# Outputs of the pair path stored by row tile from 128 partitions, four transfers a batch, in place of two transfers of 64 partitions

## Chip, cores and metric

The kernel runs on one core of one Trainium2 chip. The metric is the device time of one execution in microseconds (us); lower is better. A core has five engines with queues of their own: PE (matmul; weight loads are shown apart as PEld), DVE (vector), ACT (scalar), POOL (GpSimd) and SP (which here only issues transfers). Transfers between the large memory (DRAM) and the on-chip memory of 128 partitions run on 16 DMA engines that all issuers share.

## What is computed

For 8 batches of 576 rows: linear attention with 8 heads of 64 columns, and behind it an MLP mixer with a token part and a channel part.

```python
phi = lambda x: np.where(x > 0, x, np.exp(x) - 1.0) + 1.0
kv  = einsum('bhsd,bhse->bhde', phi(k), v);  z = sum(phi(k), axis=2)
x   = einsum('bhsd,bhde->bhse', phi(q), kv) / (phi(q) . z + 1e-6)   # heads side by side: [8, 576, 512]
u   = x + (relu(x^T @ w_tok1) @ w_tok2)^T                           # 576 -> 256 -> 576
out = u + relu(u @ w_ch1) @ w_ch2                                   # 512 -> 1536 -> 512, float32
```

## The kernel before

A row s of a batch is written as s = 9 p + t, with p from 0 to 63 and t from 0 to 8 (`out.rearrange("n (p t) d -> n p t d", t=9)`, called `outv`). A row tile r, from 0 to 3, holds t = 2r in partitions 0 to 63 and t = 2r + 1 in partitions 64 to 127; `half[0]` and `half[1]` are these two halves. The 64 rows with t = 8 of each batch are the tail; tails of two batches share one tile and are stored on their own (`mm4_tail_put`).

The eight batches overlap. Every step is registered under a name by `put(name, function, ...)`, and the string `ORDER` (L66), written out by hand, lists the names in the order in which their instructions are issued; each engine works through its own instructions in that order and waits on semaphores where data are not ready. Names begin with the batch. `L` is an input load on SP's queue (L228), `qT` and `uT` are DMA transposes on SP's queue (L335, L489), `kx`, `qx`, `ka`, `qa`, `v` prepare phi and v on ACT and DVE (L252, L256, L275), `K`, `n`, `f`, `g` are matmuls of attention and of the token part, `x` and `p` those of the channel part (L928 and L970), which are done as seven products of half-size blocks with sums before and after.

Batch 0 stores its row tiles from `obuf`, a float32 buffer of six slots of 512 columns, by `mm4_put` (names `0o0`, `0o1`): for each pair of row tiles one transfer from each half, L764. Batches 1 to 6 take the pair path: a product holds two row tiles at once, so slot r of `obuf` (slots 0 to 3) holds row tile r, and the steps write quarters. `pair_end` (names `eZ`, `eW`, `eY`, `eX`, on DVE, L1064) adds PSUM and u into rows d and d + 2, columns half c, with (d, c) = Z (0, 0), W (1, 1), Y (0, 1), X (1, 0). `pair_copy` (`c0` to `c2`, ACT, L1058) copies a product to a buffer `part[i]` (these buffers lie in `q_raw`, `w` and `part`), and `pair_more` (`hZ`, `hY`, `hW`, POOL, L1071) adds it to Z, Y or W. Then `pair_put` (name `o`, POOL, L1075) stores all four tiles, one transfer from each half:

```python
for e in range(2):
    nc.gpsimd.dma_start(out=outv[n, :, e:e + 7:2], in_=slots(f"{n}P", 4)[half[e]])
```

Rows 0 and 2 (d = 0) are complete after `hZ` and `hY`, rows 1 and 3 after `hW` and `eX`. The slots 0 to 3 are the same for all batches of the pair path, so the `e` steps of a batch wait until the transfers of the batch before have read them. Batch 7 has a path of its own: it adds into `obuf` by L984 and L1031 and stores through SP and ACT at the end.

Of the kernel before, what the change touches and what calls it, by code (L numbers as in the profile page):

```python
# [64 lines left out]

ORDER = """A2 A0 A1 A3 A4 A5 A6 A8 A9 A7 A10 A12 A13 A14 A11 A16 A17 A15 A19 A18 A21 A20 A22 A23 A24 A25 A26 A27 A28 A29  # L66
A30 A33 A31 A32 A35 A34 A36 A37 A38 1Lk0 A39 1Lk1 1Lv1 A40 1Lq0 A41 1Lq1 A42 1Lv0 A43 0ma0 At2 0ma1 At3 0ma3
0mb1 0mb0 0ma6 0r0 0mb3 0r1 1ka0 0ma7 1kx0 0ma2 0ma8 0mb6 1kb0 0mb2 0r3 0mb8 0mb7 0r6 0r8 0ma4 0r7 G21 0gt
1kx1 G22 0ma9 0gv 0ma10 0mb4 1ka1 0r2 0ma5 0r4 G11 0mb10 1kb1 0mb5 0r10 G23 0mb9 0r5 0ma11 0mb11 1qa0 1qx0 B0
0r9 0q0 B1 0r11 1qb0 B2 1qx1 1qa1 1Q00 1Q01 0q1 1Qc01 1v0 1Qc00 0q2 1qb1 1v1 1Q10 1Q11 1K 1Qc11 2Lq0 ws02  # L70
1Qc10 0q3 2Lq1 1Kc0 1Kc1 2Lv0 ws04 1n20 1n01 2Lk0 1nc20 0q4 2Lk1 1nc01 2Lv1 1n10 0q5 1nc10 1n00 0q6 1nc00 1n11
0q7 1nc11 2qx0 1n21 ws14 0q8 1nc21 1f0 2qx1 2qa0 1f1 wt2 3Lq0 G24 0q9 1fr1 2qb0 1fr0 0q10 2qa1 2v0 G12 1h01
2qb1 1h00 1hu01 2qT1 ws00 0q11 1hu00 0z1 2kx0 1h10 2qT0 ws10 0z0 1h11 1hu10 1t0 1hu11 1t1 3Lv0 ws24 1g2 1tc1
1tc0 1t2 3Lq1 1t3 1gu2 1ma9 1tc3 ws12 0z2 1ma1 1ma5 1tc2 1ma4 0z3 1mb1 2v1 0o1 1mb5 1r1 1ma7 2ka0 2kx1 1mb7
G01 3Lk0 1ma10 0o0 G03 3qx0 1mb4 2kb0 0ut 1ma2 2ka1 1r4 1mb10 wt0 3Lk1 1mb2 1r7 1ma3 3Lv1 1r2 2kb1 1mb9 1r10
1ma8 3qa0 0uc 1mb8 1r5 ws20 1r9 2K 1r8 1mb3 2Kc0 2Kc1 3qb0 1ma6 1r3 2n ws30 2nd 1mb6 T00 2o0 ws34 1r6 2n1
1ma11 Tr00 2o1 ws22 1mb11 2ne 3v0 2n0 1ma0 1mb0 3qa1 T01 4Lv0 1r0 2n2 ws32 1r11 1p10 3qx1 2f0 1w13 G02 Tr01
4Lq1 1w10 1p11 3kx1 3qb1 1p20 3ka0 3kx0 2f1 1w20 G14 2fr0 4Lk0 T02 1w23 3qT1 1w30 1p50 Tr02 3kb0 1p51 2fr1
3qT0 1c0 1w40 1p21 4qx1 2g1 3ka1 1c2 1eZ 1p60 3v1 G13 1p61 2gu1 2g0 1c1 3kb1 2uT1 1p31 2gu0 4kx0 1p30 3K 4qa1
2uT0 1p71 3Kc1 1eY 3Kc0 4v0 1p70 4qb1 4Lv1 4Lq0 3n 1hY 1eW 4Lk1 U00 3ne 5Lv0 3nd 1hZ U01 3n2 U02 3o0 1hW 3n1  # L80
1p40 3n0 2x01 2x11 2s1 3o1 1p41 V0 2y11 2x02 2y01 2s2 1eX 2x15 2x21 2s3 1o 2x12 2y21 2x16 2y12 2x06 2y16 2s4
2x05 2y06 2y02 2x17 2y15 4qa0 2x26 4qx0 2x25 2y17 2x07 G04 3f0 2y25 4qb0 2y05 4ka0 2y26 4qT1 2x14 2x03 2y07
2y14 2x13 3fr0 4qT0 3f1 2y13 4kb0 2x27 5Lq0 3fr1 2y03 2x23 5Lk0 2x04 2y27 2x22 2y04 4ka1 2x24 4kx1 2y22 3gt
3g1 2y23 2y24 2w10 2p20 2w12 2p10 2w20 3gu1 2p50 2p11 2w22 3uT1 2p51 3gt1 2c0 3g0 4v1 4kb1 2w30 2p60 2p61 3gu0
2p21 2c1 3gt0 3uT0 4K 2eZ 2p70 4Kc1 2c2 2w40 3ut 2p71 4Kc0 4n 2eW 5Lq1 2p30 4nd 2hW 5Lk1 4ne 2p31 5Lv1 4n0
2p41 2hZ 4o0 4n1 2p40 3x11 3s1 3x21 4o1 3y11 3s2 3x01 4n2 5kx0 3x16 3x12 2eY 3y21 T12 3s3 5v0 2eX 2hY 3x15
3y12 3x05 3y16 3x02 5ka0 2o 3y01 3x26 3y02 6Lk0 3x25 3x06 5kb0 3y25 W0 3x22 3y26 5ka1 3x23 3y06 3x17 3y22 3y15
3x27 3s4 3y05 3x07 3y17 5kx1 T11 3y27 3x03 3y07 Tr12 6Lk1 3x14 Tr11 3y03 3x24 5kb1 3x13 3y24 4f0 3y13 5qx0
5qa0 4f1 3y14 3y23 4fr0 5qb0 3x04 4fr1 T10 3w12 3y04 5qa1 4g0 Tr10 3w10 5v1 4g1 4gu0 5qx1 3p20 4gu1 4uT0 5K
6kx1 3p21 3w20 4uT1 5qb1 3p10 5Kc1 6kx0 3w22 3p11 5qT1 3eZ 3p50 3c0 6ka1 3p51 5Kc0 5qT0 3w40 U10 3c2 3w30 U11  # L90
6Lq0 6Lq1 6kb1 U12 4s1 6ka0 3p31 V1 3p30 7Lk0 4s2 6Lv1 3p61 3eY 6Lv0 3p60 6kb0 7Lk1 5n 3c1 5nd 3hY 3p71 5ne
3p70 5n0 3hZ 4x02 5o0 3eW 4x01 4x21 5n2 4y01 3hW 3p40 4y21 4y02 4x06 6qx0 5n1 4x05 4x26 4y06 6qa1 3p41 4y05
5o1 4x11 4s3 4x03 3eX 4y11 4x25 4y26 4s4 3o 4x07 4y03 6qx1 4x12 4y07 4x16 4x27 4y25 4y12 4x04 4y16 6qb1 5f0
4y04 6qa0 6v0 4x15 4y27 4x23 4w10 4y15 4x17 6qb0 5fr0 4x22 4y17 4x13 6qT0 4x24 4y23 4x14 4y24 4y13 6qT1 5f1
4y14 4y22 6v1 7ka1 4p20 4w12 4p21 5fr1 4w20 5g1 4w22 4p10 5gu1 4p11 5g0 4w40 5uT1 4c0 4eZ 5gt 6K 5gu0 4hZ 4p50
6Kc1 6Kc0 5gt1 5uT0 7kx1 4p51 5gt0 4p60 4c2 4w30 7Lv0 6n 7kx0 7Lq0 7kb1 4p61 7Lq1 6ne 7Lv1 4p30 6nd 4c1 6n2
4p31 4p71 6n0 4p70 4eY 5x11 6o1 5x02 6o0 5y11 5s1 5x12 4eW 5x01 5s2 5x15 5y01 4hW 6n1 4p40 7v0 5x16 5y12 4p41
5y16 7ka0 5x06 5y15 5s3 5x21 5y02 7F12 5x13 5y21 4eX 4hY 5x17 5y06 5x05 5y17 5x26 5y05 7kb0 4o 5x07 5y26 5x25
5y13 5x03 5y25 5s4 5x27 7qa0 7qx0 6f0 5y07 7v1 7qb0 5x14 6f1 7qa1 7qx1 5y27 5x04 6fr0 5y03 5x22 6fr1 5x23 7qb1
5y14 5x24 5y22 5y04 7qT1 7K 5y23 5p10 7Kc1 7Kc0 5w10 7qT0 5y24 6g0 5w30 6g1 5w12 5w20 5p20 6gu1 5p50 5p11 5w22  # L100
6uT1 6gu0 5p21 5c0 5p51 5eZ 6uT0 5p60 5c2 5w40 7n 5hZ 7nd 5p61 7ne 5p31 7n1 5c1 7F15 5p30 7o1 7o0 5p70 7n2
5p71 6s1 5eY 6x21 6x01 6s2 5hY 7n0 6x11 6y01 6x12 6y11 6x06 6y21 6s3 6x15 5eW 6y06 6x16 6x02 5hW 6y16 6x05
6y02 5p40 6y12 7F14 6x26 6s4 6y15 6x17 7F11 6x25 6y26 6x07 7F10 6y05 5p41 6y25 W1 6x13 5eX 6x03 6y07 6x23 7F13
6x27 6y03 6x22 5o 6x04 6y22 7f0 6y17 6y23 7f1 7fr0 6y27 6y04 6x14 6y13 7fr1 6x24 6y14 6w30 7g0 6y24 6w10 6p10
7gu0 7g1 6w12 7uT0 6p11 6w20 6p50 6w22 6c0 5ut 6p20 7gu1 6p51 7F2 7uT1 7gt 6p61 7gt0 6p60 6w40 7x12 6c1 7gt1
6p21 6c2 7F4 7ut 6p71 6eZ 7x11 6p70 7s1 6hZ 7x02 6eW 7x01 6p30 7y01 6hW 6p31 7y11 7y02 7x05 7s2 6p40 7y12 7y05
7s3 7x06 7s4 7x16 7y06 6eY 7x03 6p41 6hY 7x15 6eX 7c1 7y15 7F3 6o 7y16 7x21 7cr1 7y03 7x13 7y21 7x17 7c5 7y17
7x07 7x26 7y07 7x22 7y26 7x25 7y22 7x14 7x27 7y14 7x04 7y25 7c4 7y04 7y27 7cr5 7x23 7w10 7cr4 7x24 7y23 7c3
7y24 7w30 7w20 7c2 7y13 7w14 7c0 7cr2 7w12 7w40 7cr3 7p50 7w34 7cr0 7w22 7p51 7w24 7w42 7p10 7w44 7ts1 7p11
7ta1 7R11 7R51 7p20 7w32 7t5 7R10 7ts2 7R50 7p61 7tb1 7p31 7R61 7ts4 7R20 7p30 7R31 7tr5 7p60 7tr1 7ts3 7p71  # L110
7R60 7p21 7t6 7R21 7R30 7p70 7R71 7D200 7tr6 7t3 7D711 7D710 7ta2 7D201 7tr3 7D210 7R70 7tb2 7p41 7D311 7tr2
7D310 7t7 7D211 7R41 7td20 7p40 7D411 7tr7 7D410 7t4 7td21 7R40 7D700 7D701 7tr4 7td70 7td71"""


@with_exitstack
def kernel(
# [20 lines left out]
    nc = tc.nc  # L137
# [23 lines left out]
    def bank(name):  # L161
        return psum[:, BANK[name]]
# [47 lines left out]
    half = [slice(0, 64), slice(64, 128)]  # L210
# [27 lines left out]
    def put(name, fn, *a):  # L238
        assert name not in tok, name
        tok[name] = lambda: fn(*a)  # L240
# [4 lines left out]
    def slots(name, m):  # L245
        return obuf[:, SLOT[name]:SLOT[name] + m]
# [504 lines left out]

    outv = out.rearrange("n (p t) d -> n p t d", t=T)

    def mm4_read(p, t):
        b, r = divmod(t, R)
        if t < 8:
            o, y = slots(f"0o{r // 2}", 2)[:, r % 2], u[b][:, r, :]
        else:
            o, y = slots(f"V{p}", 1)[:, 0], ut[p % 2]
        nc.vector.tensor_tensor(out=o, in0=bank(f"U{p}{t}"), in1=y, op=ALU.add)  # L760

    def mm4_put(i):
        for e in range(2):
            nc.gpsimd.dma_start(out=outv[0, :, 4 * i + e:4 * i + e + 3:2],  # L764
                                in_=slots(f"0o{i}", 2)[half[e]])

    def mm4_tail_put(p):
        for b in range(2):
# [10 lines left out]
    for r in range(R):  # L779
        put(f"0z{r}", mm4_read, 0, r)  # L780
    for i in range(2):
        put(f"0o{i}", mm4_put, i)
    for p in range(2):
        for i in range(3):
            put(f"U{p}{i}", mm4, p, 8, range(4 * i, 4 * i + 4))
        put(f"V{p}", mm4_read, p, 8)
        put(f"W{p}", mm4_tail_put, p)
# [282 lines left out]
        o = slots(f"{n}P", 4)[:, d::2, HC[c]]  # L1070
        nc.gpsimd.tensor_tensor(out=o, in0=o, in1=part[i], op=ALU.add)  # L1071

    def pair_put(n):
        for e in range(2):
            nc.gpsimd.dma_start(out=outv[n, :, e:e + 7:2], in_=slots(f"{n}P", 4)[half[e]])  # L1075

    for n in range(1, B - 1):
        for i in range(3):
            put(f"{n}c{i}", pair_copy, n, i)
        for z in "WZYX":  # L1080
            put(f"{n}e{z}", pair_end, n, z)
        for z, i in zip("WZY", (2, 0, 1)):
            put(f"{n}h{z}", pair_more, n, z, i)
        put(f"{n}o", pair_put, n)


    zeros = raw["v", 1].rearrange("p j f -> p (j f)")[:, 0:512]
# [110 lines left out]
```

## Time and profile before

| | us |
|---|---|
| median of 3 runs (244.76, 245.8, 245.11) | 245.11 |
| span of the profiled execution, first to last instruction | 243.4 |
| PE busy | 233.1 |
| DVE busy | 211.5 |
| ACT busy | 136.4 |
| POOL busy | 81.2 |
| one put of `pair_put` on POOL (12 of them), from issue to landing, median | 6.0 |
| issue of one such put, busy time of POOL | 0.634 |

The profile shows one execution; no separate time is given for it beside its span. Queue q0 is that of the transfers which POOL issues, q1 and q10 those of SP and ACT. DMA shares are means over the 16 engines. "Landing" is when the semaphore of a transfer reaches its full count. A wait is put down to what ended it last; "issue" is time in which an engine waited for nothing that the profile shows. The granted clock of PE is full in all forty slices.

### The profile page before, as it was taken

What the parts mean: (1) busy time and instruction counts of PE and PEld (TensorE: products, weight loads), DVE (VectorE), ACT (ScalarE), POOL (GpSimd) and SP (SyncE); (2) the same over time, 40 slices, a digit from 0 to 9 for tenths busy, and PEclk for the clock granted to TensorE, in tenths of its full rate; (3) what the DMA queues carried; (4) which work ended last, traced back from release to release, by engine and by line L of the source; (5) the groups of instructions that cost most, each with busy time, mean ns of one, the idle gap of its engine ahead of it and who ended that gap; (6) DMA issues with size and microseconds to landing.
All of it is one profiled execution on the core that took longest, in us unless ns stands there. A gap on an engine that the chain in (4) does not pass through costs nothing.

```text
span 243.4 us, 6361 instructions
## 1 busy us (share of the span) xinstructions
PE 233.1 (96%) x2597; PEld 174.2 (72%) x2616; DVE 211.5 (87%) x387; ACT 136.4 (56%) x224; POOL 81.2 (33%) x88
## 2 busy tenths in 40 slices
PE   7889989999999999999999999999999999999991
PEld 3575445464677686789867887688778867888881
DVE  5955786999999989999999999999999599867661
ACT  4773782669788277327994297448923542347000
POOL 8870044076910620035200520206015810440730
PEclk9999999999999999999999999999999999999999
DMA  6999989999979989978948989495782285143035
GB/s 230 278 202 260 317 260 234 409 283 286 365 225 198 270 265 161 247 97 305 285 127 175 370 262 200 82 260 178 161 138 40 44 171 112 24 91 81 3 80 180
DMA packets 49805, 48.42 MB, mean 199 GB/s; under 512 B 30064, under 2 KB 35568, under 8 KB 49776
## 3 DMA queue, kind: packets, MB, share of 16 engines
q1 hardware_dynamic: 41664, 35.00, 51.3%
q0 software_dynamic: 7472, 12.22, 25.5%
q10 hardware_dynamic: 640, 0.79, 1.0%
q8 instruction: 20, 0.33, 0.6%
q14 instruction: 9, 0.07, 0.1%
HBM read 35.85 MB, written 9.44 MB: 186 GB/s over the span
## 4 chain that ended last, share of the span: by engine, by line
PE 84%; DMA 9%; POOL 3%; issue 1%; DVE 1%; SPq 1%; POOLq 0%; DVEq 0%
PE ps L970 27%; PE ps L928 23%; PE ps L747 6%; PE ps L448 6%; DMA q_raw<-in_q_dram 5%; PE ps L459 4%; PE ps L686 4%; DMA wc<-in_moe_w_ch_dram 4%; PE ps L711 2%; PE ps L733 2%; PE ps L302 2%; PE ps L1024 2%; PE ps L387 2%; POOL qT L1111 1%; POOL cr L233 1%
## 5 line engine op out<-in xcount | busy, mean ns | idle before, releaser
L970 PE MATMUL ps<-k_raw,v_raw 128*128 128x256 bf16 x252 | 31.8, 273 | 0.0
L943 ACT COPY v_raw<-ps 128x512 f32<-128x512 f32 x30 | 17.0, 595 | 22.7 <-PE ps L928 21.5
L970 PEld LDWEIGHTS <-cr 128*128 128x128 bf16 x252 | 24.4, 98 | 4.8
L970 PEld LDWEIGHTS <-v_raw 128*128 128x128 bf16 x252 | 24.1, 98 | 3.8 <-issue 0.4
L928 PEld LDWEIGHTS <-swc 128*128 128x128 bf16 x240 | 23.4, 98 | 3.1
L681 DVE CUSTOM_DVE_ANT_0 cr<-ps,v_raw 128x512 bf16<-128x512 f32 x30 | 20.1, 684 | 4.5 <-PE ps L928 2.5
L928 PEld LDWEIGHTS <-wc 128*128 128x128 bf16 x216 | 21.1, 98 | 3.6
L928 PE MATMUL ps<-crt,swc 128*128 128x256 bf16 x180 | 23.1, 273 | 0.0
L252 ACT ACTIVATE e<-q_raw 128x1152 bf16<-128x1152 f32 x16 | 18.7, 1167 | 6.7 <-DMA q_raw<-in_q_dram 6.7
L686 PE MATMUL ps<-uT,wc 128*128 128x512 bf16 x91 | 21.6, 379 | 0.4 <-issue 0.2
L970 PE MATMUL ps<-wc,cr 128*128 128x256 bf16 x168 | 21.6, 273 | 0.0
L1071 POOL TENSOR_TENSOR obuf<-obuf,w 128x512 f32<-128x512 f32 x6 | 8.2, 1360 | 38.6 <-ACT w L1058 19.5
L252 ACT ACTIVATE e<-k_raw 128x1152 bf16<-128x1152 f32 x16 | 18.5, 1166 | 3.2 <-DMA k_raw<-in_k_dram 2.6
L1071 POOL TENSOR_TENSOR obuf<-obuf,q_raw 128x512 f32<-128x512 f32 x6 | 8.2, 1374 | 35.6 <-DVE obuf L1064 35.6
L928 PE MATMUL ps<-uT,wc 128*128 128x256 bf16 x144 | 19.5, 273 | 0.0
L1064 DVE TENSOR_TENSOR obuf<-ps,u 128x512 f32<-128x512 f32 x24 | 16.4, 685 | 2.5 <-PE ps L970 2.4
L1071 POOL TENSOR_TENSOR obuf<-obuf,part 128x512 f32<-128x512 f32 x6 | 7.7, 1289 | 26.5 <-DVE dens L400 18.5
L413 DVE TENSOR_TENSOR x<-ps,dens 128x768 bf16<-128x768 f32 x18 | 16.6, 930 | 0.0
L686 PEld LDWEIGHTS <-wc 128*128 128x128 bf16 x96 | 8.9, 98 | 10.0 <-issue 0.6
L470 DVE TENSOR_TENSOR u<-ps,x 128x1024 bf16<-128x1024 f32 x12 | 14.6, 1220 | 0.1
L836 DVE TENSOR_TENSOR v_raw<-cr 128x512 bf16<-128x512 bf16 (+3 forms) x24 | 14.5, 620 | 0.0
L448 PE MATMUL ps<-x,w 128*128 128x512 bf16 x50 | 13.9, 379 | 0.3
(168 smaller groups left out, 514.3 us busy)
## 6 DMA issues: line engine op xcount, KB each, us to landing
k_raw<-in_k_dram SPq DMA_DIRECT2D x16, 576.0 KB, 6.8
q_raw<-in_q_dram SPq DMA_DIRECT2D x16, 576.0 KB, 6.3
v_raw<-in_v_dram SPq DMA_DIRECT2D x14, 576.0 KB, 7.6
out_dram<-obuf POOLq DMA_DIRECT2D x12, 512.0 KB, 6.0
wc<-in_moe_w_ch_dram POOLq DMA_DIRECT2D x8, 384.0 KB, 9.3
out_dram<-obuf POOLq DMA_DIRECT2D x4, 256.0 KB, 7.3
cr<-in_v_dram POOLq DMA_DIRECT2D x2, 288.0 KB, 7.6
out_dram<-obuf POOLq DMA_DIRECT2D x4, 128.0 KB, 4.8
```

Source lines behind the costliest of these rows:

```text
L252: nc.scalar.activation(out=ebuf[EBUF[f"{n}{nm}{c}"]], in_=f, func=AF.Exp)
L413: nc.vector.tensor_tensor(out=xv[:, :, rc0:rc0 + 3], in0=nd_tile(n, m)[:, :, k0:k0 + 6, 0:D].rearrange("p i (q a) d -> p i q a d", a=2), i ...
L448: nc.tensor.matmul(out=banks(f"{n}f")[:, mt], lhsT=w1t[:, b, ms] if r == R else w1[:, r, ms], rhs=x[b][:, r, :], start=(r == 0), stop=(r = ...
L470: nc.vector.tensor_tensor(out=u[b][:, rs], in0=banks(f"{n}g{i}"), in1=x[b][:, rs], op=ALU.add)
L681: nc.vector._custom_dve(TENSOR_ADD_SAT, out=o, in0=ps, in1=c, s0=3.4028234663852886e38, s1=0.0)
L686: nc.tensor.matmul(out=bank(f"{n}m{mc}"), lhsT=wc1[:, kj, 128 * mc:128 * mc + 128], rhs=uTj[b][:, kj] if n < 2 - U1 else uT[b][:, :, kj], ...
L747: nc.tensor.matmul(out=bank(f"U{p}{t}"), lhsT=crt[:, kc, :] if t == 8 else cr[b][:, kc, 128 * r:128 * r + 128], rhs=wc2[:, kc, :], start=( ...
L928: nc.tensor.matmul(out=ps[:, j], lhsT=lhs[:, k_, 128 * j:128 * (j + 1)], rhs=rhs[:, :, k_], start=(first and j == 0 and k_ == 0), stop=(k_ ...
L943: nc.scalar.copy(out={1: c1, 6: c6, 5: c5}[i], in_=ps)
L970: nc.tensor.matmul(out=ps, lhsT=lhs[:, k_], rhs=rhs[:, k_], start=(first and not skip and k_ == 0), stop=(k_ == KH - 1), skip_group_check= ...
L1064: nc.vector.tensor_tensor(out=slots(f"{n}P", 4)[:, d::2, HC[c]], in0=pair_tile(n, "X" if z == "W" else z), in1=u[n % 2][:, d::2, HC[c]], o ...
L1071: nc.gpsimd.tensor_tensor(out=o, in0=o, in1=part[i], op=ALU.add)
```

## The change

One function now stores one row tile from all 128 partitions: the output side walks the two halves e, then p, then the columns. Batch 0 calls it for its four tiles (four transfers, as before), batches 1 to 6 for each tile as well (four transfers in place of two). For the pair path the name `o` becomes `oa` (rows 0 and 2) and `ob` (rows 1 and 3).

```diff
+    def put_rows(n, r, rows):
+        nc.gpsimd.dma_start(out=outv[n, :, 2 * r:2 * r + 2].rearrange("p e d -> e p d"), in_=rows)
+
     def mm4_put(i):
-        for e in range(2):
-            nc.gpsimd.dma_start(out=outv[0, :, 4 * i + e:4 * i + e + 3:2],
-                                in_=slots(f"0o{i}", 2)[half[e]])
+        for r in (2 * i, 2 * i + 1):
+            put_rows(0, r, slots(f"0o{i}", 2)[:, r % 2])
...
-    def pair_put(n):
-        for e in range(2):
-            nc.gpsimd.dma_start(out=outv[n, :, e:e + 7:2], in_=slots(f"{n}P", 4)[half[e]])
+    def pair_put(n, d):
+        for r in (d, d + 2):
+            put_rows(n, r, slots(f"{n}P", 4)[:, r])
...
-        put(f"{n}o", pair_put, n)
+        for d in range(2):
+            put(f"{n}o{'ab'[d]}", pair_put, n, d)
```

In `ORDER` each `no` (n from 1 to 6) becomes `nob` in the same place, and `noa` is put directly behind the later of `nhZ` and `nhY`; all other names keep their order. For batch 3:

```diff
-3p70 5n0 3hZ 4x02 5o0 3eW ...  3eX 4y11 4x25 4y26 4s4 3o 4x07
+3p70 5n0 3hZ 3oa 4x02 5o0 3eW ...  3eX 4y11 4x25 4y26 4s4 3ob 4x07
```

On POOL the batches 1, 3 and 5 now have two puts, the addition `hW`, then two puts (in batch 5 other work stands between as well); the batches 2, 4 and 6 have four puts in a row where two stood. The shape of the output side goes from 64x4x512 (batch 0: 64x2x512) to 2x64x512, that of the input side from 64 to 128 partitions. The order of instructions on PE, DVE, ACT and SP is the same in both kernels.

## The prediction

> **What bounds the kernel now.** I read the page first, then PE's waits after 55 us, the timeline of POOL, the DMA view in stretches where one kind of transfer runs alone, and last the landings against their readers. From the page: PE's row of busy time, the forty slices of PE and of the DMA engines, and the two queues that carry nearly all bytes.
>
> ```profile
> PE 233.1 (96%) x2597; PEld 174.2 (72%) x2616; DVE 211.5 (87%) x387; ACT 136.4 (56%) x224; POOL 81.2 (33%) x88
> PE   7889989999999999999999999999999999999991
> DMA  6999989999979989978948989495782285143035
> q1 hardware_dynamic: 41664, 35.00, 51.3%
> q0 software_dynamic: 7472, 12.22, 25.5%
> ```
>
> PE is at nine tenths or more in every slice from the tenth to the one before last; a slice is 6.1 us. The DMA engines are nearly as full up to about 140 us, but full is not late. Whether PE waits for a transfer is told by its waits, here of matmuls from 55 to 239 us and of weight loads from 66 to 239 us (in all, times, longest):
>
> ```profile
> PE ps L747 <- issue: 0.2, 1, 0.2
> PE ps L686 <- issue: 0.2, 1, 0.2
> ...
> PEld L302 <- issue: 1.3, 5, 0.4
> PEld L387 <- issue: 1.1, 5, 0.2
> ```
>
> No matmul there waits for a DMA, for DVE, ACT or POOL; what is left is "issue". The first output put is issued at 55.5 us, so from the first instruction that this change touches, PE already runs through. The chain that ended last is 84% PE, and its DMA parts (wc and q_raw) end at 32 us. The change can shorten a transfer, but no wait of PE is there for it to end.
>
> **The change, part by part.** The profiled span is 243.4 us; of the three runs the median is 245.11, so about 1.7 us lie outside the span, and no separate time is listed for the profiled execution. I add to 243.4 and carry the 1.7.
>
> *The transfers themselves.* Two stretches show one kind each: 215 to 223 us, only the two puts of batch 6 (64 partitions each); 159 to 168 us, nearly only loads of 128 partitions.
>
> ```profile
> DMA packets 288, 1.05 MB, mean 131 GB/s; under 512 B 32, under 2 KB 32, under 8 KB 288
> q0 software_dynamic: 288, 1.05, 61.8%
> ...
> DMA packets 1159, 2.39 MB, mean 265 GB/s; under 512 B 134, under 2 KB 134, under 8 KB 1158
> q1 hardware_dynamic: 1158, 2.37, 78.2%
> ```
>
> Without the small ones the puts are 256 packets of 4096 B and take 61.8% of 16 engines for 8 us, 79.1 us in all: 309 ns each, 13.3 bytes per ns. The loads are 1024 packets of 2304 B in 78.2% of 16 times 9 us, 112.6 us: 110 ns, 20.9 bytes per ns. The slices agree: the puts never pass 287 GB/s, the loads reach 451. So a batch's 1 MB holds each of 16 engines now for 16 packets of 309 ns, 4.9 us; at the loads' rate a 4096 B packet would take 196 ns and the batch 3.1 us. For puts from 128 partitions no row exists; the bounds are 196 ns and 309 ns, and I take 196, the row that shares the partition count. Gain: 1.8 us of transfer time for each of six batches and batch 0, all of it behind PE. Worth nothing: no PE wait ends there.
>
> [...]
>
> *Issues on POOL.* Four puts a batch in place of two. Rows now: 634 ns (64x4x512, L1075, 12 of them), 606 to 1156 ns (64x2x512, L764), 542 to 1052 ns (64x512, L769). I take 634: 2.54 us a batch in place of 1.27, so 1.27 more (bounds 0.9 and 3.4), 7.6 us over six batches on an engine that is busy a third of the time. Batch 0 keeps four issues. What hides it is seen in POOL's timeline, batch 3 (idle time before, and its releaser, in brackets):
>
> ```profile
> 136.35 1.26 POOL L1071 TENSOR_TENSOR obuf<-obuf,w 128x512 f32<-128x512 f32 x1 [19.48 <-ACT w L1058]
> 137.58 1.26 POOL L1071 TENSOR_TENSOR obuf<-obuf,q_raw 128x512 f32<-128x512 f32 x1
> 138.80 1.28 POOL L1071 TENSOR_TENSOR obuf<-obuf,part 128x512 f32<-128x512 f32 x1
> 143.36 1.28 POOL L1075 DMA_DIRECT2D out_dram<-obuf  x2 [3.28 <-DVE q_raw L885]
> 155.52 1.27 POOL L1071 TENSOR_TENSOR obuf<-obuf,q_raw 128x512 f32<-128x512 f32 x1 [10.87 <-DVE obuf L1064]
> ```
>
> In batches 1, 3 and 5 the first two puts stand ahead of the last addition (hW), which goes back by 1.27 us; behind it POOL idles 3.59 us (batch 1) and 3.28 us (batch 3) before the second half, so that starts when it does now. In batch 5 the slip is 0.3 us (hW started at 188.86, the puts end near 189.2), and the sums of L869 behind it feed matmuls after 212 us. In batches 2, 4 and 6 the four puts stand together and POOL then idles 19.5, 12.0 and 10.1 us (in batch 2 after the two puts of the tail). The next use of `part` is a copy of the next batch, 17 us or more later. Without that cover each slip would cost at most its 1.27 us. The early puts wait for POOL's own two additions only, so nothing queues behind a foreign wait; SP, DVE, ACT and PE keep their order.
>
> *Buffers.* The slots of obuf are rewritten by DVE (L1064) at 105.08, 128.74, 154.70 and 181.08 us; the puts before them land at 96.38, 122.19, 150.54 and 175.74. The smallest cover is 4.2 us, and it grows, as rows 0 and 2, which are rewritten first, leave earlier. The last batch writes from 227.55 us, the puts of batch 6 land at 222.16: 5.4 us.
>
> *Neighbours.* Early puts of batches 1 and 3 (82.9 and 138.8 us) now run beside input loads that end at 89.2 and 144.8. At 16 engines each pair adds 1.6 us (half of 3.1); the nearest readers are at 89.72 (load landed at 86.28) and at 145.80 (landed at 143.40): covers 3.4 and 2.4 us. So nothing. The sum is 243.4 + 0 = 243.4, and 245.1 us with the rest.
>
> **Rivals.** *A, slower: each put on few engines.* The program now gives the output side as 2x64x512 against 128 rows of obuf; every transfer before has 64 or 128 rows outermost on both sides, so no row tells how 2 x 64 is spread. If it went by the 2, each engine would carry 128 KB: 32 packets, 6.3 us at 196 ns and 9.9 us at 309. The first put of batch 6 lands after 4.4 us, of which its 8 packets on each engine are 2.5, so some 1.9 us are fixed, so a put lands after 8.2 us (11.8). The narrowest place is the transpose of qT for batch 6:
>
> ```profile
> L335 SPq DMA_TRANSPOSE qT<-qp x2: 1299/1805/2311, 175.0 to 176.4; - x2
> DMA to landing us min/median/max: 4.5/4.7/4.9
> 181.96 0.79 PE L387 MATMUL ps<-kvbd,qT 64*128 64x65 bf16 x40
> ```
>
> The second, issued at 176.38, lands at 181.3, and PE needs it at 181.96: 0.7 us of cover. The puts of batch 4 land now at 175.74; under A the fourth, issued near 170.6, lands at 178.8 (182.4), beside both transposes. Where transposes had full company (71 to 80 us) they took 6.2 to 6.7 us; so qT would land at 182.6 to 183.1, PE late by 0.6 to 1.2 us, or by about 2 at 309 ns. In batch 3 the load that lands at 143.40 has 2.7 us left when the put gets going at 140.7, and at half share lands near 146.1; packet by packet (110 ns against 196) its share is 36%, and it lands near 148.2. ACT reads it at 145.80 and is late by 0.3 to 2.4 us, of which the 1.1 us that it idles before 149.0 is cover. Together 0.6 to 3.3 us; I take 1.7, near the middle, as neither delay need reach PE whole: 246.8 us. It decides once a transpose takes over 5.6 us. Against it: puts that rotate over the engines leave most of them free, and POOL issues all of them within 2.5 us. [...]
>
> *B, the same two engines every time.* Then a batch's four puts queue up for 25 us (4 times 6.3) and meet every transpose of the next batch: some 5 us for each of five batches, 270 us. Nothing in the trace speaks for it.
>
> *C, faster.* With the engines less full, PE's "issue" waits (0.4 us, and 4.0 us of weight loads after 66 us) could shrink, if they are late instructions. A third of them gives 243.7 us. Against it: they recur in fixed places, L302, L387 and L478, whatever DMA does.
>
> *D, the half rate stays* (309 ns from 128 partitions too). The puts then take 4.9 us as now: 245.1 us.
>
> **How the numbers follow.** Forecast 0.46, A 0.36, B 0.05, C 0.09, D 0.04. A measurement of this kernel tells about 0.5%, 1.2 us, from no change. Forecast and D lie within it, and 0.06 of A, where the covers take the delay; 0.30 of A and B are slower; C is faster. That gives 0.09, 0.56, 0.35. Likeliest is 245.1 us; its own range is 244.4 to 245.9, about the spread of the runs. To hold 8 in 10 the range goes up over most of A, to 248.5, and down to 244.3, which leaves out B, most of C and the end of A.
>
> **What would show it.** Right: software packets in the last put window near 200 ns per 4096 B with slices near 400 GB/s, PE's waits still "issue" alone, POOL's issues near 0.63 us. A is right if puts land after 8 us or more while the DMA share in 217 to 223 us stays far below half, and PE or PEld waits for qT at L387. The forecast is wrong if any wait of PE after 55 us names a DMA, or ACT or DVE behind one.

## The result and the profile after

The changed kernel takes 267.1 us (median of 6 runs, 260.26 to 271.73) against 245.31 (6 runs, 244.76 to 245.8). The ratio of the compared runs is 1.0669, with a 95% interval of 1.0605 to 1.0733: slower by 6.7%, and outside the predicted range (244.3 to 248.5 us). The profiled execution took 265.25 us and is one of the longer ones, while the ratio rests on the two shortest (260.26 and 263.75 us); medians, here and below, are of all runs, and ratios compare with runs of before taken alongside. The accounts below are made against its own span of 263.5 us.

The page of the kernel after, the rows that answer to those of before (busy time; forty slices of 6.6 us; the queues; the shares of the chain that ended last):

```profile
PE 242.8 (92%) x2616; PEld 177.3 (67%) x2616; DVE 216.3 (82%) x387; ACT 136.4 (52%) x224; POOL 92.5 (35%) x100
PE   7889989999989999979978999799958999999992
PEclk9999999999999999999997999989995999999999
DMA  7999999999869979997798939991594145404126
...
q1 hardware_dynamic: 41664, 35.00, 53.5%
q0 software_dynamic: 20208, 12.33, 23.8%
...
PE 45%; DMA 33%; DVE 9%; POOL 4%; ACT 4%; issue 2%; SPq 1%; DVEq 0%; POOLq 0%; ACTq 0%
```

Four things differ from before. PE has slices at five to eight tenths in the middle, where it had nine. The granted clock, full before, is down in a few slices, each time together with or right behind such a hole. Queue q0 moves the same bytes in 20208 packets, where 7472 did before. And the chain is 33% DMA; before, its DMA parts ended at 32 us.

What PE's matmuls wait for from 55 to 262 us (in all, times, longest; the three largest rows):

```profile
PE ps L387 <- DMA qT<-qp: 5.7, 2, 3.8
PE ps L972 <- ACT part L1060: 2.2, 1, 2.2
PE ps L930 <- DMA uT<-u: 1.7, 2, 1.5
```

The same view of before named "issue" alone. The second row is a DMA too, one step back: PE waits for ACT's copy (L1060), which stands behind ACT's phi (L252), and that sat idle for 4.41 us, up to 135 us, until a load of `k_raw` landed, 12.2 us after its issue at 122.7.

The last put window, four puts of batch 6 with nothing else on the DMA engines (234 to 249 us):

```profile
DMA packets 2113, 1.08 MB, mean 72 GB/s; under 512 B 1856, under 2 KB 1856, under 8 KB 2112
out_dram<-obuf POOLq DMA_DIRECT2D x4, 256.0 KB, 11.1
```

Before, 288 packets stood here; now there are 2112. Four puts are 4 x 64 packets of 4096 B, so most of the others are tiny: 4 x 448 of 8 B. 448 is 14 x 32. The trace does not name the engine of a packet, so it is an estimate from these counts that each put has 32 data packets on each of two engines, and 32 packets of 8 B on each of the other fourteen; the rates of single puts below fit it. Over the whole run a 256 KB put lands after 12.3 us (median of 28); a put of twice the size took 6.0 before. A data packet itself has become faster, 159 ns (median) against 324.

**Where the 20.1 us of span went.** PE's idle time rises from 10.3 us (243.4 less 233.1) to 20.7 (263.5 less 242.8), by 10.4; its busy time rises by 9.7. The second part is mostly the clock. The timeline of PE around the longest wait (start, busy time, instructions, idle time before):

```profile
193.09 1.47 PE L972 MATMUL ps<-k_raw,v_raw 128*128 128x256 bf16 x12
198.41 1.28 PE L387 MATMUL ps<-kvbd,qT 64*128 64x65 bf16 x40 [3.85 <-DMA qT<-qp]
199.63 1.46 PE L972 MATMUL ps<-k_raw,v_raw 128*128 128x256 bf16 x6
```

Twelve matmuls of L972 take 1.47 us ahead of the wait; behind it six take 1.46. The windows view gives the granted clock there as 0.50 from 197.7 to 204.5 us, and likewise from 139.7 to 143.1 (behind a wait of 2.24 us) and from 170.4 to 173.8 (behind one of 1.86). These 13.6 us at half clock cost up to 6.8 us. About 3 us of the longer busy time is not itemised. Part of it is that the trace of before lacks 19 of PE's 2616 matmuls, so its busy time is counted low: in the version with 64 outermost below, whose trace has all 2616, it is 234.3 us against 233.1.

### The profile page after: what moved, and what is told of

It reads as the page before. It is cut to its first block, busy times and chain, and to the rows that moved or that the text cites. A ratio compares the mean times of both kernels' runs of the same rounds, so it can differ in the third digit from the quotient of the medians.

```text
span 263.5 us, 6402 instructions
## 1 busy us (share of the span) xinstructions
PE 242.8 (92%) x2616; PEld 177.3 (67%) x2616; DVE 216.3 (82%) x387; ACT 136.4 (52%) x224; POOL 92.5 (35%) x100
## 3 DMA queue, kind: packets, MB, share of 16 engines
q0 software_dynamic: 20208, 12.33, 23.8%
## 4 chain that ended last, share of the span: by engine, by line
PE 45%; DMA 33%; DVE 9%; POOL 4%; ACT 4%; issue 2%; SPq 1%; DVEq 0%; POOLq 0%; ACTq 0%
PE ps L972 14%; PE ps L930 14%; DMA k_raw<-in_k_dram 10%; DMA qT<-qp 6%; PE ps L747 5%; DMA q_raw<-in_q_dram 5%; DMA uT<-u 4%; DMA out_dram<-obuf 4%; DMA wc<-in_moe_w_ch_dram 4%; PE ps L448 3%; DVE cr L681 2%; PE ps L459 2%; DVE y L256 2%; ACT e L252 2%; PE ps L387 1%
## 5 line engine op out<-in xcount | busy, mean ns | idle before, releaser
L972 PE MATMUL ps<-k_raw,v_raw 128*128 128x256 bf16 x252 | 34.4, 287 | 0.0
L972 PEld LDWEIGHTS <-v_raw 128*128 128x128 bf16 x252 | 25.5, 104 | 5.2 <-issue 0.4
L972 PEld LDWEIGHTS <-cr 128*128 128x128 bf16 x252 | 24.4, 98 | 4.8
L755 POOL DMA_DIRECT2D out_dram<-obuf x28 | 23.6, 846 | 8.4 <-DVE cr L681 3.0
L930 PEld LDWEIGHTS <-swc 128*128 128x128 bf16 x240 | 23.4, 98 | 3.7 <-issue 0.5
L930 PEld LDWEIGHTS <-wc 128*128 128x128 bf16 x216 | 20.9, 98 | 6.6 <-DMA uT<-u 2.0
L681 DVE CUSTOM_DVE_ANT_0 cr<-ps,v_raw 128x512 bf16<-128x512 f32 x30 | 20.1, 682 | 5.9 <-PE ps L930 3.7
L930 PE MATMUL ps<-crt,swc 128*128 128x256 bf16 x180 | 23.1, 272 | 0.3 <-DVE x L422 0.3
L252 ACT ACTIVATE e<-k_raw 128x1152 bf16<-128x1152 f32 x16 | 18.6, 1166 | 9.3 <-DMA k_raw<-in_k_dram 9.3
L686 PE MATMUL ps<-uT,wc 128*128 128x512 bf16 x96 | 22.6, 379 | 0.7 <-DVE x L422 0.5
L1066 DVE TENSOR_TENSOR obuf<-ps,u 128x512 f32<-128x512 f32 x24 | 16.4, 685 | 8.1 <-PE ps L972 5.5
L252 ACT ACTIVATE e<-q_raw 128x1152 bf16<-128x1152 f32 x16 | 18.7, 1166 | 7.6 <-DVE den L363 5.8
L972 PE MATMUL ps<-wc,cr 128*128 128x256 bf16 x168 | 21.6, 273 | 0.0
L930 PE MATMUL ps<-uT,wc 128*128 128x256 bf16 x144 | 19.5, 273 | 1.7 <-DMA uT<-u 1.7
L1073 POOL TENSOR_TENSOR obuf<-obuf,q_raw 128x512 f32<-128x512 f32 x6 | 8.8, 1458 | 35.1 <-DVE obuf L1066 35.1
L686 PEld LDWEIGHTS <-wc 128*128 128x128 bf16 x96 | 8.9, 98 | 10.9 <-issue 1.8
L972 PE MATMUL ps<-wc,q_raw 128*128 128x256 bf16 x84 | 13.7, 326 | 2.5 <-ACT part L1060 2.2
L256 DVE TENSOR_SCALAR y<-k_raw 128x1152 bf16<-128x1152 f32 x16 | 12.5, 782 | 4.1 <-DMA k_raw<-in_k_dram 3.9
## 6 DMA issues: line engine op xcount, KB each, us to landing
out_dram<-obuf POOLq DMA_DIRECT2D x28, 256.0 KB, 12.3
out_dram<-obuf POOLq DMA_DIRECT2D x4, 128.0 KB, 10.3
```

Of the source, the lines that this page charges most:

```text
L252: nc.scalar.activation(out=ebuf[EBUF[f"{n}{nm}{c}"]], in_=f, func=AF.Exp)
L256: nc.vector.tensor_scalar(out=ybuf[YBUF[f"{n}{nm}{c}"]], in0=f, scalar1=1.0, scalar2=1.0, op0=ALU.add, op1=ALU.max)
L681: nc.vector._custom_dve(TENSOR_ADD_SAT, out=o, in0=ps, in1=c, s0=3.4028234663852886e38, s1=0.0)
L686: nc.tensor.matmul(out=bank(f"{n}m{mc}"), lhsT=wc1[:, kj, 128 * mc:128 * mc + 128], rhs=uTj[b][:, kj] if n < 2 - U1 else uT[b][:, :, kj], ...
L755: nc.gpsimd.dma_start(out=outv[n, :, 2 * r:2 * r + 2].rearrange("p e d -> e p d"), in_=rows)
L930: nc.tensor.matmul(out=ps[:, j], lhsT=lhs[:, k_, 128 * j:128 * (j + 1)], rhs=rhs[:, :, k_], start=(first and j == 0 and k_ == 0), stop=(k_ ...
```

## The experiments

Theory S (spread): a put goes to as many DMA engines as its output side has rows outermost, two here, and everything that shares those engines lands late. Rival theories: the early place of `oa` and the additional issues on POOL do it; or the mere number of transfers. All kernels are edits of the changed kernel, but for two: one has nothing but transfers, and one is the kernel before with the new puts in batch 0.

**The spread by itself.** First the outermost size of the output side, everything else as changed. With 64 outermost:

```diff
-        nc.gpsimd.dma_start(out=outv[n, :, 2 * r:2 * r + 2].rearrange("p e d -> e p d"), in_=rows)
+        nc.gpsimd.dma_start(out=outv[n, :, 2 * r:2 * r + 2], in_=rows)
```

This takes the same bytes to the same rows as a set, but partition q now lands in the row with p = q//2 and t = 2r + q%2. What this version and the next two leave out is the right place of each row: they show what the shape costs, and are no replacement.

> As the changed kernel, but the output side of each put is walked p first (64x2x512) in place of the two halves first (2x64x512): same source, same number, place and size of puts, same rows written as a set, though partition q now lands in row 9(q//2)+2r+q%2, so rows are placed otherwise than the reference. Theory SPREAD (a put runs on as many of the 16 DMA engines as the outermost size of its output side, 2, and the long puts delay the transposes and loads that PE waits for): 244.5 to 246 us, no packets of 8 B, puts landing in 3.5 to 5 us, software packets of 4096 B near 160 ns, no wait of PE on qT or uT. Rival ISSUE (four issues on POOL a batch, of 0.85 us each, and the early pair of puts are what costs): as the changed kernel, 260 to 267 us. Rival SOURCE (reading 128 partitions in one put costs): 260 to 267 us too.

Measured: 246.81 us, ratio 1.0066 (1.0045 to 1.0086), a little above the 244.5 to 246 us expected. Page:

```profile
q0 software_dynamic: 7664, 12.23, 20.0%
out_dram<-obuf POOLq DMA_DIRECT2D x28, 256.0 KB, 3.1
```

The tiny packets are gone, a put lands after 3.1 us (3.5 to 5 expected), and no matmul after 55 us waits for a DMA. Of the 6.7%, 6.0 points go with this one expression. The sizes in between, 8 and 4:

```diff
+        nc.gpsimd.dma_start(out=outv[n, 16 * r:16 * r + 16, 0:8].rearrange("p e d -> e p d"),
+                            in_=rows)
```

> As the changed kernel, but the output side of each put is 8x16x512 (tile r goes to p from 16r, all t below 8, t first): same bytes and the same set of rows, placed otherwise than the reference. SPREAD: 8 engines carry 8 packets of 4096 B each, 1.3 us of data; the other 8 carry 8 packets of 8 B each, that is 64 per put, if the 448 per put of the changed kernel are 14 engines times 32. Puts land in about 4.5 us and the time is 244.5 to 247 us. ISSUE and SOURCE: 260 to 267 us.

```diff
+        nc.gpsimd.dma_start(out=outv[n, 32 * (r // 2):32 * (r // 2) + 32, 4 * (r % 2):4 * (r % 2) + 4].rearrange(
+                "p e d -> e p d"), in_=rows)
```

> As the changed kernel, but the output side of each put is 4x32x512 (tile r goes to 32 values of p and 4 of t, t first): same bytes and set of rows, placed otherwise than the reference. SPREAD: 4 engines carry 16 packets of 4096 B each, 2.6 us of data, and the other 12 carry 16 packets of 8 B, 192 per put; puts land in 6 to 8 us and the time lies between, 246 to 254 us. ISSUE and SOURCE: 260 to 267 us.

Measured: 247.71 us for 8 (1.0075, 1.0029 to 1.0121), 257.36 us for 4 (1.0545, 1.0498 to 1.0592). Their pages, 8 first:

```profile
out_dram<-obuf POOLq DMA_DIRECT2D x28, 256.0 KB, 5.9
```
```profile
out_dram<-obuf POOLq DMA_DIRECT2D x28, 256.0 KB, 8.9
```

Landing grows with every halving of the spread, 3.1, 5.9, 8.9, 12.3 us, and the number of tiny packets in a put is 0, 64, 192, 448, which is 8 for each engine that is left out by the estimate above, then 16, then 32. The time does not follow evenly: up to 5.9 us the covers of the kernel take nearly all of it, and at 8.9 us most of the loss is there. In the profile with 4, PE waits 2.7 us behind the `k_raw` load and 2.1 us for `qT`. Times and landings of both lie above what was expected (244.5 to 247 us and 246 to 254, landing after 4.5 us and 6 to 8).

**The transfer alone.** The same forms on an idle chip; the kernel does nothing but puts of one constant tile.

```diff
+    alone(nc.gpsimd, two, 0)        # three puts, one after the other has landed
+    alone(nc.gpsimd, four, 1)
+    alone(nc.gpsimd, eight, 2)
+    alone(nc.gpsimd, full, 3)
+    halves(4, False)                # the transfer of before: 64 partitions, 512 KB
+    alone(nc.sync, two, 5)
+    alone(nc.sync, full, 6)
+    burst(nc.gpsimd, two, 7)        # four puts without a wait between them
+    burst(nc.gpsimd, full, 0)
+    halves(1, True)
+    burst(nc.sync, two, 2)
```

> Only puts, nothing computed: 256 KB from 128 partitions in four output shapes (2x64, 4x32, 8x16, 64x2 rows of 512) from POOL's queue, each three times with nothing else under way, then half puts of 512 KB, then the shapes 2x64 and 64x2 from SP's queue, then bursts of four puts, of two halves, and of four from SP. SPREAD: landing alone from POOL falls with the outermost size: data takes 32, 16, 8 and 4 packets of 160 ns on an engine (5.1, 2.6, 1.3, 0.6 us) over a fixed part of 1.5 to 3 us; packets of 8 B are 448, 192, 64 and 0 per put. If the pairs of engines go round, the last of four 2x64 puts in a burst lands about when the first does plus three issues; if they are always the same two, it lands 15 us later. From SP no theory has a row yet: if the lowest engines are taken each time, the burst of four takes 20 us or more. ISSUE and SOURCE: landing does not depend on the output shape.

The DMA view, by windows of this kernel (puts, size, median time to landing in us): three puts each of 2, 4, 8 and 64 outermost, then the burst of four with 2.

```profile
out_dram<-big POOLq DMA_DIRECT2D x3, 256.0 KB, 9.0
...
out_dram<-big POOLq DMA_DIRECT2D x3, 256.0 KB, 6.6
...
out_dram<-big POOLq DMA_DIRECT2D x3, 256.0 KB, 4.2
...
out_dram<-big POOLq DMA_DIRECT2D x3, 256.0 KB, 2.4
...
out_dram<-big POOLq DMA_DIRECT2D x4, 256.0 KB, 11.3
```

With nobody else on the engines a put of the changed form takes 9.0 us, and a put of 64 x 2 takes 2.4; the 9.0 us are more than the 6.6 to 8.1 us that the expectation adds up to. In the burst the four landed after 9.1, 9.5, 13.1 and 13.8 us: POOL's puts overlap, so they do not queue up fourfold, though they are not free of each other either. From SP it is otherwise: data moved until 21.3 us after the last issue. The engines, which the trace does not name, are estimated from the rates. One put of 2 x 64 by itself moves 50 to 55 GB/s, and two engines with a packet of 4096 B in 159 ns each would move 51.5. POOL's burst reaches 156 GB/s, three times that, so by this estimate its puts are on different pairs of engines. SP's burst never passes 53, which is what four puts on one pair would give. The prediction's rival B described just that, for another queue than the kernel uses. A transfer of the old form (64 partitions, 512 KB) takes 4.2 us alone, with a median packet of 301 ns, against 159 to 171 ns for packets of the same 4096 B in POOL's forms of 128 partitions: alone too, a packet of the old form takes 1.8 to 1.9 times as long as one of these.

**The places.** What if `oa` had stayed beside `ob`, still with 2 outermost:

```diff
-3p70 5n0 3hZ 3oa 4x02 ...  4s4 3ob 4x07
+3p70 5n0 3hZ 4x02 ...  4s4 3oa 3ob 4x07
```

> The changed kernel with oa directly ahead of ob in every batch: four puts in a row of 2x64x512, none ahead of hW. SPREAD: as long as in the changed kernel, only later: 255 to 267 us. A rival that blames the early place of oa (loads met at 83 and 139 us, hW put back): 246 to 250 us.

Measured: 268.78 us, 1.085 (1.0806 to 1.0893), a little above the 255 to 267 us expected. PE's waits of its profile, 55 to 266 us:

```profile
PE ps L930 <- DMA uT<-u: 6.2, 2, 4.4
PE ps L387 <- DMA qT<-qp: 6.1, 2, 4.3
PE ps L972 <- ACT part L1060: 4.3, 1, 4.3
```

Same readers, longer waits: the early place is not the cause, it even softens the loss, probably because part of the bytes leave sooner. Now the opposite, the early places with the old kind of transfer, four halves of 64 partitions:

```diff
     def pair_put(n, d):
-        for r in (d, d + 2):
-            put_rows(n, r, slots(f"{n}P", 4)[:, r])
+        for e in range(2):
+            nc.gpsimd.dma_start(out=outv[n, :, 2 * d + e:2 * d + e + 5:4],
+                                in_=slots(f"{n}P", 4)[half[e], d::2])
```

Batch 0 is back to its two halves of before as well.

> The change without its shape: four puts a batch at the places of oa and ob, but each from one half of 64 partitions and two slots (64x2x512 on both sides, output as the reference). ISSUE: 260 us or more, as the issues and their places are those of the changed kernel. SPREAD and SOURCE: 244.5 to 246.5 us, packets of 4096 B near 325 ns as before the change, no packets of 8 B, POOL issues near 0.63 to 0.78 us.

Measured: 246.35 us, 1.0047 (1.003 to 1.0065). Four issues and the early place cost about half a per cent, from halves as with 64 outermost (0.66%), and between 55 and 240 us its profile lists no wait of a matmul. One thing came out otherwise than expected: POOL's packets of 4096 B were to stay near 325 ns, and their median is 159. The queue's row:

```profile
q0 software_dynamic: 7664, 12.23, 22.5%
```

It had 25.5% before and 20.0% with 64 outermost. So 64 partitions alone do not make every packet slow; with four smaller transfers, again from 64 partitions, the median is that of the new form (159 ns). Why is not shown here.

**The batches.** Only batch 0 with the new form, batches 1 to 6 as before (against the kernel before; `put_rows` is that of the change):

```diff
     def mm4_put(i):
-        for e in range(2):
-            nc.gpsimd.dma_start(out=outv[0, :, 4 * i + e:4 * i + e + 3:2],
-                                in_=slots(f"0o{i}", 2)[half[e]])
+        for r in (2 * i, 2 * i + 1):
+            put_rows(0, r, slots(f"0o{i}", 2)[:, r % 2])
```

> The kernel before with the new puts in batch 0 alone (four of 2x64x512), the pair path as before. SPREAD: these four start near 55 us beside input loads, land after 12 to 18 us and cost what PE stood still near 65 and 75 us in the changed kernel, 1 to 3 us: 246 to 248 us. ISSUE: no issue is added, so 245.3 us.

Measured: 245.94 us, 1.002 (0.9996 to 1.0044). That is a little less than the 246 to 248 us expected. The interval holds 1; by it the part of batch 0 in the loss is 0.4% at most.

The prediction's rival A placed the loss at the transposes for batches 5 and 6. Two of the waits in the changed kernel are there (L387). So batches 3 and 4, whose puts stand ahead of those transposes, were given the wide form and all others the narrow one:

```diff
+        o = outv[n, :, 2 * r:2 * r + 2]
+        nc.gpsimd.dma_start(out=o if n in (3, 4) else o.rearrange("p e d -> e p d"), in_=rows)
```

> The changed kernel with the output side 64x2x512 in batches 3 and 4 alone (their rows placed otherwise than the reference), 2x64x512 in the others. SPREAD says that each batch's puts pay where they meet transposes and loads: PE's gaps at L387 before the matmuls of batches 5 and 6 (1.9 and 3.8 us in the changed kernel) go, with the half clock beside them, those near 112 and 137 us stay; 250 to 257 us. A theory by which the total of transfer time counts, wherever it lies, takes a third to a half of the loss away evenly and leaves the two gaps smaller, but there.

Measured: 260.1 us, 1.0598 (1.0554 to 1.0643); 256.67 us in the profiled execution. Its PE waits, 55 to 262 us:

```profile
PE ps L931 <- DMA uT<-u: 3.8, 2, 2.3
PE ps L973 <- ACT part L1061: 2.5, 1, 2.5
PE ps L973 <- DVE obuf L987: 1.8, 2, 1.3
```

Both waits at L387 are gone, and the total fell by only 0.7 points of 6.7, less than expected. Other waits take over: `uT` again (2.3 us up to 112.8 us, and newly 1.5 us up to 215.1, for the last batch), and the rewriting of `obuf` in batch 7, where DVE waited 1.99 us for puts of batch 6. That cover had been counted at 5.4 us. Removing waits one by one does not give their sum back while the narrow puts of four other batches remain.

**The last half per cent.** In the kernel with 64 outermost one step differs from before. Its POOL and DVE timelines, batch 3:

```profile
140.08 1.29 POOL L755 DMA_DIRECT2D out_dram<-obuf  x2 [0.30 <-POOL obuf L1073]
141.39 1.27 POOL L1073 TENSOR_TENSOR obuf<-obuf,part 128x512 f32<-128x512 f32 x1
```
```profile
141.84 1.45 DVE L256 TENSOR_SCALAR y<-q_raw 128x1152 bf16<-128x1152 f32 x1
```

The two early puts push the addition `hW` back by 1.3 us, so that it runs together with DVE's L256, which took 0.75 us before and now takes 1.45. ACT's steps that wait for PE's L930 come 0.94 us later than before ahead of it (139.69 against 138.75 us) and 1.34 us later behind it (150.34 against 149.00), so PE loses about 0.4 us there, an estimate from these starts. With four halves it is the same: L256 takes 1.41 us. To take the overlap away, four halves again, with the early pair behind `hW` in batches 1, 3 and 5:

```diff
-3p70 5n0 3hZ 3oa 4x02 5o0 3eW ... 3hW 3p40
+3p70 5n0 3hZ 4x02 5o0 3eW ... 3hW 3oa 3p40
```

Batch 0 has its two halves here too.

> As four_halves (four puts of 64 partitions, two slots), but in batches 1, 3 and 5 the early pair stands directly behind hW in place of ahead of it. Theory PORT (what is left of the loss, 0.5 to 0.7%, comes from hW of batch 3, which the puts ahead of it put back by 1.3 us, on to DVE's L256, which then takes 1.45 us in place of 0.75): L256 at about 141 us back at 0.75 us, hW in its old place, and 0.5 us less than four_halves, 245.2 to 245.8 us. Rival COUNT (twelve more transfers cost by themselves): 246.3 us as four_halves.

Measured: 245.66 us, 1.0018 (1.0003 to 1.0033). The timelines show `hW` in its old place behind the other two additions, and DVE's step short again:

```profile
139.64 1.26 POOL L1074 TENSOR_TENSOR obuf<-obuf,part 128x512 f32<-128x512 f32 x1
```
```profile
141.73 0.75 DVE L256 TENSOR_SCALAR y<-q_raw 128x1152 bf16<-128x1152 f32 x1
```

So 0.2 to 0.3% of the 0.5% was this kind of collision: the step on PE gives 0.4 us, 0.2%, and the two ratios differ by 0.29 points, though their intervals just touch and the edit moves the early pair of three batches, not of batch 3 alone. What the traces show is the overlap and its price: 0.75 us became 1.45 beside an addition of 1.27 us, and is 0.75 again without it. Why DVE's step is longer there is not shown.

Last the form that should be best, 64 outermost and all four puts late, so that no addition is delayed:

```diff
+        nc.gpsimd.dma_start(out=outv[n, :, 2 * r:2 * r + 2], in_=rows)
...
-3p70 5n0 3hZ 3oa 4x02 ...  4s4 3ob 4x07
+3p70 5n0 3hZ 4x02 ...  4s4 3oa 3ob 4x07
```

> As rows_64_2 (output side 64x2x512, rows placed otherwise than the reference, all 16 engines), but oa stands directly ahead of ob in all batches, so nothing is put ahead of hW. PORT: 245.2 to 245.7 us, L256 in batch 3 at 0.75 us. COUNT: 246.5 us or more. A theory that half the transfer time is worth something to this kernel: under 244.5 us.

Measured: 246.01 us, 1.0024 (1.0009 to 1.0039), a little above the 245.2 to 245.7 us expected. The rows stand in other places here too. Queue q0 needs 20.2% of the engines in place of 25.5%, and PE's matmul waits, 55 to 239 us, are the two of before: "issue" at L686 and L747, 0.2 us each.

Faster transfers bring nothing here. Where the remaining 0.2% is, was not found: the profiled span is 243.4 us, as before, and PE's course is the same step by step from 142 to 158 us. None of these versions beats the kernel before.

## Why the prediction was wrong

*What bounds the kernel* was right: PE does, and shorter transfers end no wait. The version with 64 outermost and late puts shows it, with 3.7 us to landing and no gain.

*The transfers.* The rate was better than both its bounds, and the form was wrong. 196 ns for 4096 B from 128 partitions had been taken, with 309 as the other bound; 159 to 171 were measured (medians). With 64 outermost the last put window has 256 such packets in 35.3% of 16 engines for 8 us, 177 ns each, so that a batch occupies 16 engines for 2.8 us. But the changed kernel has each put's data on two engines, by count and rate of packets (448 of 8 B a put, 50 to 55 GB/s alone), and the forecast's "16 engines" is the step that failed: with it the 3.1 us a batch, the covers and the term of nothing for the neighbours fell. A put takes 9.0 us alone and 12.3 in the kernel in place of 2.4 and 3.1, and PE waits for the transposes and loads beside it. The doubt was in the text, as rival A, with the right mechanism and a chance of 0.36. No row of before told how an outermost size of 2 is spread; the runs here do: with 2, 4, 8 and 64 outermost a put lands after 12.3, 8.9, 5.9 and 3.1 us.

*Rival A's price* (0.6 to 3.3 us, 246.8 us in all) was mis-sized too, in three terms.
- The landing. 8.2 us was 32 packets of 196 ns and 1.9 us fixed. The packets were faster, yet a put alone lands after 9.0 us, so some 3.7 us come on top of 32 x 165 ns, against 1.7 on top of 4 x 165 for 64 outermost. Whether the tiny packets make the difference is open: SP's burst of four in the same form had 8 packets under 512 B in all, and moved at up to 53 GB/s, where one put of POOL by itself moves at 50 to 55. In the company of the other transfers it became 12.3 us.
- The places. One transpose and one load of batch 3 were priced. The two transposes of `qT` landed after 6.4 to 10.0 us where 4.5 to 4.9 had been, far over the 5.6 us from which A was to decide, and so did `uT` (6.8 to 7.3 us for the pair issued at 105.3 and 106.8, 4.2 to 4.7 before), the `qT` of the batch before (8.9 to 9.5 us) and another load, that of `k_raw` for batch 6 (12.2 us, 5.7 before). "Neither delay need reach PE whole" was wrong: 3.85 us at once reached it.
- The clock. Half clock behind the waits (0.50 for 13.6 us) was in no step, and costs up to 6.8 us of the 20.1.

*Issues on POOL* were hidden, as said, but took 846 ns on average in this form (634 taken, bounds 542 to 1156); with 64 outermost they are back at 663. "Each slip would cost at most its 1.27 us", behind the cover, missed that `hW` moves onto a DVE step (0.75 us to 1.45): about 0.4 us on PE.

*Buffers.* The covers of 4.2 us and 5.4 us held with 64 outermost, where nothing waits for a put. With 2 outermost both were used up: in the changed kernel DVE waits for puts from `obuf` for 1.78 us ahead of L1066 (195.48 us) and for 0.82 us ahead of L986 (248.50 us, batch 7), and in the version with batches 3 and 4 wide for 1.99 us in batch 7.

*The other rivals.* By the rates of the bursts B did not happen on POOL's queue (156 GB/s), and did on SP's (53 at most). D, whose "half rate" is the 309 ns of the puts before, fell: packets from 128 partitions took 159 ns (median). C fell: the "issue" waits of matmuls are the same two of 0.2 us with 64 outermost and late puts, where queue q0 needs 20.2% of the engines in place of 25.5%. What was to show the forecast wrong, a wait of PE that names a DMA, is the first row of the view.

## What to carry to other kernels

Before a store is reshaped, look at the outermost size of its output side: with 2 there, 128 partitions on the input side brought no spread here (12.3 us to landing), and other transfers paid as well (the two transposes of `qT` took 6.4 to 10.0 us in place of 4.5 to 4.9). The form that keeps the many rows outermost (64 x 2 in place of 2 x 64) writes as many bytes and landed after 3.1 us in place of 12.3. It is not free, though: it takes neighbouring partitions to neighbouring rows, so the tile would have to hold the row of p and e in partition 2p + e from the start, which no run here tries. And price a late transfer by all its later neighbours, not by the narrowest cover alone.

## What was not expected of the hardware

- PE's granted clock fell to 0.50 for 3.41 us, or twice that, and it did so by steps of a grid: each half-clock stretch after 55 us, in the five profiles that have one, lasts one or two steps of 3.41 us, and the stretches of one profile lie whole steps apart (in the changed kernel they begin at 139.7, 170.4 and 197.7 us, 9 and 8 steps apart), wherever the waits are. A step of the changed kernel and the one behind it, then a step of the version with 4 outermost (start:end, length, PE's busy time, then the other engines; the third figure from the end is the granted clock):

```profile
136.28:139.69 3.41, 1.17 (x9) 0.69 (x8) 3.41 (x7) 2.75 (x5) 0.00 (x0) 1.00 0.90 200
139.69:143.10 3.41, 3.41 (x19) 2.41 (x17) 1.75 (x4) 0.00 (x0) 0.00 (x0) 0.50 0.95 277
...
131.32:134.74 3.42, 1.75 (x9) 0.68 (x7) 3.11 (x5) 3.05 (x4) 0.00 (x0) 1.00 0.96 213
```

Of the steps at full clock up to PE's last instruction, those with 1.58 us of PE work or less (1.17, 1.55 and 0.26 in the changed kernel, 1.46 with only batch 0 narrow, 1.58 with 4 outermost) were followed by half clock, and those with 1.75 or more were not. So in these profiles the length of a wait alone does not decide, and PE was not idle for the whole of a step ahead of half clock: it worked for up to 1.58 us of it. With 4 outermost, the wait of 2.7 us fell over two steps (1.75 and 2.38 us of work) and cost no clock, while the shorter one of 2.1 us did.

- A put with 2, 4 or 8 outermost sent 448, 192 or 64 packets of 8 B when POOL issued it, which is 32, 16 or 8 for each engine that, by the estimate above, carries no data. SP's four puts with 2 outermost had 8 packets under 512 B in all, POOL's four had 1856.
- The rates of the bursts (156 GB/s from POOL, at most 53 from SP) fit puts of POOL on different engines and puts of SP on the same two, an estimate, as the trace names no engine: four equal puts took 13.8 us to the last landing from the one, and data until 21.3 us after the last issue from the other.
